# Nyström attention into a sticky top-1 MoE: the own expert of two batches chosen from the mean of C v, the first batch's steps in a new list

## The chip, the cores and the metric

The kernel runs on one core of a Trainium2 chip. The metric is the device time of one execution in microseconds; the span of the profile is the part of it in which instructions run. TensorE (PE) multiplies matrices, VectorE (DVE) does sums, transpositions and two-input arithmetic, ScalarE (ACT) exponentials and copies, GpSimd (POOL) further arithmetic, and SyncE (SP) and some of the others start DMAs.

## The reference

Eight batches with eight heads, 576 tokens and 64 columns a head. The landmarks are means of 18 tokens each, 32 a head. `sm` is a softmax over the last axis.

```python
A  = sm(q, k_lm)            # 576 x 32 a head
Bm = sm(q_lm, k_lm)         # 32 x 32
C  = sm(q_lm, k)            # 32 x 576
Z = Bm.T / (norm1(Bm) * norminf(Bm) + 1e-06)
for _ in range(6):
    Z = 2 * Z - Z @ Bm @ Z
x = A @ Z @ C @ v           # heads side by side: 512 columns a token
logits = x @ w_gate; local = sigmoid(x @ w_local)
# token by token: e = argmax(logits[s]) where s == 0 or local[s] < 0.5,
# else the expert of the token before
p = softmax(logits[s])
out[s] = p[e] * (relu(x[s] @ w1[e]) @ w2[e])   # 8 experts, 1024 inside
```

## The kernel before

Each batch has one "own" expert that is computed densely for all its 576 tokens; tokens of other experts are gathered into slots and computed at the end. In the kernel before, the own expert is the one that most tokens' gates name (`votes`: a matmul of `eq` with ones, a sum, then MAX and MAX_INDEX).

The product x·w1 is never made from x. With W = Z·(C v) of a head, the kernel forms G = W·w1 for each head (line 591, `w_w1`, from `wt`, the transposed W, and `raw`, the weights), 32 landmarks a head, and then multiplies the softmax A by it (line 634, `mm1`), in chunks f0 to f7 of 128 of the expert's 1024 columns; `mm2` (line 684, and 678 for the fifth block of 64 tokens) follows two chunks behind. A batch has two passes of eight chunks: 320 tokens (256 to 575), then 256 (0 to 255). Every number is split in a high and a low half (`gh` and `gl`, `ath` and `atl`, `wh` and `wl`), which makes three matmuls of each product. The high half is a cast by ACT, the low half a subtraction by DVE (or POOL for `wl`).

The first batch's attention runs alone (`first_attention`): its steps are written out in an order by hand, and the experts of batch 0 begin when it is over. The attention of each later batch runs beside the experts of the batch ahead, and a table (`SECOND` for batch 1, `PLANS` for 2 to 7) gives each step the chunk before which it is emitted; 16 chunks make a batch. `G_AT` gives the chunks at which the two halves of the next batch's G are emitted. All engines run their own instructions in order. A DMA is started from the queue of the engine that the code names.

Names in what follows: `sk` and `sq` are the sums that make landmarks (lines 210 and 218; the second behind a pair of POOL additions, line 214); `sa` is A with tokens on partitions, `at` its transposed form; `et` the Newton iterate, p0 to p5 its six products (line 383), each followed by a copy on ACT and an addition on DVE; `u` is C v and, in nine more columns a head group, C v times the gates' weights; `wc` is W scaled; `ad` is A in memory, from which slots are filled; `h` and `hx` are the hidden activations (`hx` of the fifth block). C's scores are line 250, A's are line 421, gates line 470. `keep_warm` multiplies zeros, to no result. PE's score banks and chain banks come from a pool named `one` in turn.

## Time and profile before

| what | us |
|---|---|
| median of 3 runs | 495.1 (494.94 to 495.57) |
| the profiled execution | 495.34 |
| its span | 493.4 |
| PE busy in the span | 469.5 (95%) |
| first matmul of an expert | at 38.09 |
| first matmul of batch 0's second pass | at 75.40 |
| first matmul of batch 1's first pass | at 104.70 |
| POOL, DVE, ACT busy | 229.0, 269.8, 215.2 |

Times in rows count from the start of the span. A row of a timeline gives the start, the time in which the group was busy, engine, line, operation, and tiles out<-in; what stands in brackets is the idle time of the engine ahead of it and what ended it.

### The profile page before, as it was taken

How to read it: one execution, taken by the hardware profiler on the slowest of the kernel's cores; microseconds unless marked ns; L12 is line 12 of the kernel's file. 1: busy time of each engine (PE TensorE's matmuls, PEld its weight loads, DVE VectorE, ACT ScalarE, POOL GpSimd, SP SyncE). 2: the span in 40 equal slices, each digit the busy share in tenths (PEclk: the TensorE clock that was granted, in tenths of full speed). 3: DMA queues.
4: the chain of work that ended last, by engine and by line, in shares of the span. 5: the costliest groups of instructions: out<-in, count | busy, mean ns of one | idle time of the engine just before them, and what ended most of it. 6: DMA issues, size and time to landing. Idle time of an engine off the chain costs nothing.

```text
span 493.4 us, 12117 instructions
## 1 busy us (share of the span) xinstructions
PE 469.5 (95%) x4699; PEld 341.6 (69%) x4701; DVE 269.8 (55%) x823; ACT 215.2 (44%) x562; POOL 229.0 (46%) x332
## 2 busy tenths in 40 slices
PE   7759999999999999899999999999999999999994
PEld 2425667677785677667776777677786787788773
DVE  6777785675467436845465445446553466363220
ACT  3417536373163713554253723465343613532451
POOL 6267682385067604762256703353242714352661
PEclk9958999999999999999999999999999999999999
DMA  8967542954079605961197306341721361191230
GB/s 297 389 240 246 193 145 63 389 192 145 1 257 336 195 0 193 324 229 44 37 400 243 109 11 230 131 163 62 266 104 44 101 252 37 60 316 42 62 130 19
DMA packets 38620, 82.57 MB, mean 167 GB/s; under 512 B 3180, under 2 KB 4460, under 8 KB 37793
## 3 DMA queue, kind: packets, MB, share of 16 engines
q1 hardware_dynamic: 30672, 66.22, 38.6%
q10 hardware_dynamic: 6400, 10.49, 5.9%
q0 software_dynamic: 1488, 5.07, 2.8%
q8 instruction: 38, 0.62, 0.5%
q14 instruction: 22, 0.17, 0.1%
HBM read 66.34 MB, written 15.47 MB: 166 GB/s over the span
## 4 chain that ended last, share of the span: by engine, by line
PE 80%; DVE 5%; DMA 4%; issue 4%; POOL 3%; ACT 2%; POOLq 0%; SPq 0%; ACTq 0%; DVEq 0%
PE py L684 33%; PE ph L634 20%; PE pg L678 6%; PE ph L591 3%; PE one L250 3%; DMA raw<-w 3%; PE one L421 3%; PE one L383 3%; PE one L289 2%; PE one L275 2%; POOL t L214 1%; PE one L470 1%; DMA k_t<-kT 1%; PE pg L591 1%; POOL wl L622 1%
## 5 line engine op out<-in xcount | busy, mean ns | idle before, releaser
L684 PE MATMUL py<-wh,h 128*128 128x512 f32 x528 | 170.2, 403 | 0.9 <-DVE h L646 0.6
L622 POOL TENSOR_TENSOR wl<-raw,wh 128x512 fp32r<-128x512 f32 x72 | 92.3, 1306 | 69.3 <-ACT wh L617 53.1
L684 PEld LDWEIGHTS py<-wh,h 128*128 128x128 f32 x528 | 94.7, 188 | 30.3 <-issue 9.8
L643 ACT ACTIVATE h<-ph 128x256 fp32r<-128x256 f32 (+2 forms) x136 | 54.0, 400 | 129.4 <-PE ph L634 117.7
L646 DVE SCALAR_TENSOR_TENSOR h<-ph,h 128x256 fp32r<-128x256 f32 (+1 forms) x136 | 55.9, 412 | 83.1 <-ACT h L643 82.3
L684 PE MATMUL py<-wl,h 128*128 128x512 f32 x264 | 88.8, 394 | 0.0
L634 PE MATMUL ph<-ath,gh 128*128 128x320 f32 (+1 forms) x256 | 80.4, 314 | 1.2 <-DVE h L646 1.1
L634 PE MATMUL ph<-atl,gh 128*128 128x320 f32 (+1 forms) x256 | 76.0, 297 | 0.0
L634 PE MATMUL ph<-ath,gl 128*128 128x320 f32 (+1 forms) x256 | 75.9, 296 | 0.0
L634 PEld LDWEIGHTS ph<-ath,gh 128*128 128x128 f32 x256 | 48.3, 189 | 18.5 <-issue 6.3
L684 PEld LDWEIGHTS py<-wl,h 128*128 128x128 f32 x264 | 49.5, 188 | 10.7 <-issue 0.3
L634 PEld LDWEIGHTS ph<-atl,gh 128*128 128x128 f32 x256 | 48.4, 189 | 3.9 <-issue 0.3
L634 PEld LDWEIGHTS ph<-ath,gl 128*128 128x128 f32 x256 | 48.4, 189 | 0.6 <-issue 0.5
L617 ACT CAST wh<-raw 128x512 fp32r<-128x512 f32 x72 | 42.6, 626 | 4.4 <-DMA raw<-w 3.9
L699 ACT ACTIVATE ys<-py,pall 128x512 f32<-128x512 f32 x32 | 21.0, 683 | 12.4 <-DMA out<-ys 6.9
L214 POOL TENSOR_TENSOR t<-q_t 128x288 f32<-128x288 f32 x28 | 22.5, 826 | 7.8 <-DVE sk L218 3.9
L433 POOL TENSOR_TENSOR sa<-sa,mxa 128x1152 f32<-128x1152 f32 x7 | 14.9, 2133 | 18.4 <-DVE mxa L432 18.4
L605 DVE TENSOR_TENSOR gl<-ph,gh 128x512 fp32r<-128x512 f32 (+1 forms) x19 | 12.5, 662 | 19.9 <-ACT gh L604 19.8
L708 POOL TENSOR_TENSOR ys<-ys,yl 64x512 f32<-64x512 f32 x8 | 10.2, 1281 | 28.0 <-ACT yl L706 28.0
L678 PE MATMUL pg<-wh,h 128*128 128x512 f32 x56 | 22.6, 403 | 0.0
L591 PE MATMUL ph<-raw,wt 64*32 64x512 f32 (+1 forms) x136 | 20.4, 604 | 2.1 <-DMA raw<-w 2.1
L678 PE MATMUL pg<-wl,h 128*128 128x512 f32 x56 | 22.1, 395 | 0.0
(300 smaller groups left out, 733.3 us busy)
## 6 DMA issues: line engine op xcount, KB each, us to landing
raw<-w SPq DMA_DIRECT2D x72, 256.0 KB, 5.6
raw<-w SPq DMA_DIRECT2D x17, 1024.0 KB, 7.1
v_t<-v SPq DMA_DIRECT2D x8, 1024.0 KB, 7.3
out<-ys ACTq DMA_DIRECT2D x32, 256.0 KB, 2.3
q_t<-qT SPq DMA_DIRECT2D x6, 1152.0 KB, 6.2
k_t<-kT SPq DMA_DIRECT2D x6, 1152.0 KB, 9.3
ad<-sa POOLq DMA_DIRECT2D x8, 576.0 KB, 5.3
q_t<-qT SPq DMA_DIRECT2D x4, 576.0 KB, 8.9
```

Source lines behind the costliest of these rows:

```text
L214: add = nc.gpsimd.tensor_add(t9[:, i], src[:, a + i, :, 0:9], src[:, a + i, :, 9:18])
L250: mms.append(nc.tensor.matmul(pc[hf][32 * c:32 * c + 32, 0:n], st["ql"][r, h // 2, :], st["k"][r, h // 2, 288 * hf:288 * hf + n], start=Tr ...
L433: nc.gpsimd.tensor_tensor(out=sa, in0=sa, in1=mx.unsqueeze(2).broadcast_to([P, 2 * NJ, M]), op=ALU.subtract)
L591: mm = nc.tensor.matmul(ps[g][32 * c:32 * c + 32, 0:n * P], st["wt"][r, g, 32 * c:32 * c + 32], w1[r, n * i:n * i + n, a * P:a * P + P], s ...
L617: cut = nc.scalar.copy(out=wh, in_=raw)
L622: nc.gpsimd.tensor_tensor(out=wl, in0=raw, in1=wh.bitcast(F32), op=ALU.subtract)
L634: mm = nc.tensor.matmul(hp, w[:, g, c], x[:, g, s0:s0 + n], start=(i == 0), stop=(i == 5))
L643: nc.scalar.activation(out=h[:, 0:e], in_=hp[:, 0:e], func=AF.Relu)
L646: nc.vector.scalar_tensor_tensor(out=h[:, 384:384 + m], in0=hp[:, 0:m], scalar=0.0, in1=h[:, 0:m].bitcast(F32), op0=ALU.max, op1=ALU.subtract)
L678: nc.tensor.matmul(yps[4], hs[ff][1], w, start=(ff == 0 and w is w2[ff][0]), stop=(ff == NC2 - 1 and w is w2[ff][1]))
L684: nc.tensor.matmul(yps[k], h[:, part + i * P:part + i * P + P], w, start=(f == 0 and part == 0 and w is wh), stop=(f == NC2 - 1 and part = ...
L699: nc.scalar.mul(out=ys, in_=yp, mul=st["pw"][:, k:k + 1])
```

## The change

- The own expert of batches 0 and 1 (`PICK = 2`) is no longer voted. The column mean of C v·w_gate over all landmarks and heads (a matmul with 32-bit ones, 16 columns) goes through a sum, MAX and MAX_INDEX. Gates, `mxl` and `eq` remain, since the slots and the weights p need them.
- `first_attention` is now a list of named steps, `FIRST`. The A of tokens 256 to 575, which the first pass needs, is made there (`as_1` to `sl1`, 10 blocks of 32 tokens, both head groups at once). The A of tokens 0 to 255 (`as_0` to `ad0`), the gates, the votes' rest and what follows on them are placed beside the experts of batch 0 by the chunks in `BESIDE`. The write of A to memory is in two parts.
- 36 single matmuls on zeros, z0 to z35, stand between the steps of `FIRST`; before, there were groups of 8 and 6.
- C v is emitted between the second and third Newton product, and W is scaled before the gates' columns are. PE's banks are named for each step by hand.
- `et` has another layout. The write of `wt` to memory for batch 0 is started on SP's queue in place of ACT's. One POOL addition no longer waits for the own expert of batch 0.
- `SECOND`, `PLANS` of all six batches, `G_AT`, `LATER` and `IN_ROW` have other numbers. The weights of the next own expert (`w1`) are asked for at the same entry as before for batches 1 and 3 (9.1 and 7.1), and 0.5 to 2.0 chunks later for the others.

Functions `scores_c8` and `gate_weights` are added but no batch uses them. In the new listing lines move: C's scores are line 252, A's 472 and 1072 (batch 0), G 667, `mm1` 710, `mm2` 760 and 754, gates 525, `wc` 450, landmark sums 215 and 220.

The core of the difference; of the tables, G_AT and IN_ROW stand for the rest:

```diff
+PICK = 2
...
-                add = nc.gpsimd.tensor_add(t9[:, i], src[:, a + i, :, 0:9], src[:, a + i, :, 9:18])
-                if b == 1 and a == i == 0:
-                    tc.add_manual_dep(add.ins, marks["expert of batch 0"], mybir.DependencyInfo(
-                        mybir.DependencyClass.Sync, mybir.DependencyReason.DATA), reason="not beside the first choice")
+                nc.gpsimd.tensor_add(t9[:, i], src[:, a + i, :, 0:9], src[:, a + i, :, 9:18])
...
+        (nc.scalar if b else nc.sync).dma_start(out=wtd[b], in_=st["wt"].rearrange("p g x -> p (g x)"))
...
+    def best(b, n):
+
+
+        top = sm.tile([P, E], F32, name="top")
+        nc.vector.max(out=top, in_=n)
+        marks[f"expert of batch {b}"] = nc.vector.max_index(out=regs[:, b, :], in_max=top, in_values=n).ins.name
...
+        largest(st)
+        if b < PICK:
+            return
...
+    def pick(b, st):
+
+
+
+        pt = one.tile([P, 2, E])
+        nc.tensor.matmul(pt, ones32, st["u"][:, :, D:D + E], start=True, stop=True)
+        tot = sm.tile([P, E], F32, name="tot")
+        nc.vector.reduce_sum(out=tot, in_=pt.rearrange("p g e -> p e g"), axis=AX.X)
+        best(b, tot)
 
...
+    FIRST = ("z18 q0 z4 z27 z5 c0 k0 q2 cm00 z3 b0 z15 z34 be0 k2 z29 warm z7 cm01 b1 z17 c1 z21 z8 ce0 z6 "
+             "be1 no0 z10 cm10 z1 z12 z24 nf0 z31 no1 cm11 z32 ce1 as_1 nf1 p0 e0 t0 d0 t2 t4 p1 z13 e1 v0 "
+             "cs at11 z23 d1 v1 z14 p2 e2 at01 z28 z33 ut z11 z26 d2 p3 am1 uwg e3 d3 pk w1 p4 z2 e4 d4 p5 "
+             "z22 z19 z20 ae1 z30 e5 an1 d5 nw ab1 sc1 z16 nwc nwg z25 nwt hq z9 z0 hk mq sl1 z35 mk G")
+    BESIDE = dict(as_0=0.1, at0=1.1, ad1=1.6, am0=1.6, ae0=2.6, an0=2.6, ab0=3.6, sc0=5.1, sl0=5.1, ad0=6.6,
+                  gates=3.6, votes=4.6, fresh=4.6, sticky=6.1, chosen=6.6, own=7.1)
+    G_AT = {0: (12, 14), 1: (14, 15), 2: (14, 15), 3: (14, 15)}
+    END = 4
+    LATER = (1.1, 2.0, 6.0, 8.0), (1.1, 2.6, 4.5, 6.5)
+    IN_ROW = 6
...
+        def a_scores(hf):
+            for g in range(2):
+                if hf:
+                    bank("ag"[g])
+                pa[g, hf] = one.tile([P, 512])[:, 0:32 * nh[hf]]
+            mms = []
+            for c in range(4):
+                for g in range(2):
                     r, a = rows(g, c)
-                    nc.tensor.matmul(pa[g, hf][32 * c:32 * c + 32, :], st["k"][r, a, S:S + M],
-                                     st["q"][r, a, 288 * hf:288 * hf + 288], start=True, stop=True)
+                    mms.append(nc.tensor.matmul(pa[g, hf][32 * c:32 * c + 32, :], st["k"][r, a, S:S + M],
+                                                st["q"][r, a, 256 * hf:256 * hf + 32 * nh[hf]], start=True, stop=True))
+            in_row(mms)
...
+        for k in range(36):
+            steps[f"z{k}"] = with_bank("h", lambda: keep_warm(1))
...
+        steps["w1"] = fetch
+        steps["G"] = lambda: w_w1(st, 0, 2)
...
-    G_AT = {0: (12, 15), 1: (14, 15), 2: (12, 14), 3: (11, 14)}
-    END = 4
-    LATER = (0.1, 2.5, 5.5, 6.5), (1.6, 2.1, 4.0, 5.5)
-    IN_ROW = 9
```

On DVE, just ahead of the first G: before, the sum of the votes, MAX, MAX_INDEX, then the scaling of W, `atl` for all tokens, landmark sums of batch 1, and the low half of G.

```order
L488 TENSOR_REDUCE tot<-one 128x8
L490 MAX top<-tot 128x8
L491 MAX_INDEX regs<-top,tot 128x8
L399 TENSOR_TENSOR wc<-ph,rc 128x256
L459 TENSOR_TENSOR atl<-at,ath 128x1152
L218 TENSOR_REDUCE sq<-t_559 128x64
L210 TENSOR_REDUCE sk<-k_t 128x64
L473 MEMSET lg 64x32
L605 TENSOR_TENSOR gl<-ph,gh 128x256 x2
L605 TENSOR_TENSOR gl<-py,gh 128x256 x2
```

Now, from the transposition of the first pass's A on:

```order
L1097 STREAM_TRANSPOSE at<-sa 128x640
L450 TENSOR_TENSOR wc<-ph,rc 128x256
L435 TENSOR_TENSOR wgc<-ph,rc 128x2x9
L220 TENSOR_REDUCE sq<-t_578 128x64
L215 TENSOR_REDUCE sk<-k_t 128x64
L1112 TENSOR_TENSOR atl<-at,ath 128x320 x2
L681 TENSOR_TENSOR gl<-ph,gh 128x256 x2
L681 TENSOR_TENSOR gl<-py,gh 128x256 x2
L220 TENSOR_REDUCE sq<-t_692 128x64
L215 TENSOR_REDUCE sk<-k_t 128x64
L1077 STREAM_TRANSPOSE sa<-one 128x256 x2
L722 SCALAR_TENSOR_TENSOR h<-ph,h 128x256
```

Votes and MAX_INDEX have left the place between W and G, `atl` is two pieces of 320 columns behind the landmark sums, and the transpositions of the early A scores stand behind a second pair of landmark sums and ahead of the first `h`.

On PE, from the end of the first chunk of expert matmuls on, before:

```order
L634 MATMUL ph<-ath,gl 128x320
L634 MATMUL ph<-ath,gh 128x320
L634 MATMUL ph<-atl,gh 128x320
L634 MATMUL ph<-ath,gl 128x320
L250 MATMUL one<-k_t,ql 32x288 x4
L250 MATMUL one<-k_t,ql 32x320 x4
L634 MATMUL ph<-ath,gh 128x320
L634 MATMUL ph<-atl,gh 128x320
```

And now:

```order
L710 MATMUL ph<-ath,gh 128x320
L710 MATMUL ph<-atl,gh 128x320
L710 MATMUL ph<-ath,gl 128x320
L1072 MATMUL one<-q_t,k_t 32x256 x8
L252 MATMUL one<-k_t,ql 32x288 x4
L252 MATMUL one<-k_t,ql 32x320 x4
L710 MATMUL ph<-ath,gh 128x320
L710 MATMUL ph<-atl,gh 128x320
L710 MATMUL ph<-ath,gl 128x320
```

Eight matmuls of A's scores for tokens 0 to 255 have come between chunk f0 and the scores of C for batch 1.

On PE, at the first half of G for batch 3, beside the experts of batch 2, before:

```order
L383 MATMUL one<-et 32x64 x8
L684 MATMUL py<-wh,h 128x512 x2
L684 MATMUL py<-wl,h 128x512
L591 MATMUL ph<-raw_2861,wt 32x512
L591 MATMUL pg<-raw_2861,wt 32x512
L591 MATMUL ph<-raw_2861,wt 32x512
L591 MATMUL pg<-raw_2861,wt 32x512
L591 MATMUL ph<-raw_2861,wt 32x512
L591 MATMUL pg<-raw_2861,wt 32x512
L591 MATMUL ph<-raw_2861,wt 32x512
L591 MATMUL pg<-raw_2861,wt 32x512
L634 MATMUL ph<-ath,gh 128x256
```

And now:

```order
L417 MATMUL one<-et 32x2x32 x8
L323 MATMUL one<-v_t,ect 32x64 x40
L417 MATMUL one<-et 32x2x32 x8
L667 MATMUL ph<-raw_2944,wt 32x512
L667 MATMUL pg<-raw_2944,wt 32x512
L667 MATMUL ph<-raw_2944,wt 32x512
L667 MATMUL pg<-raw_2944,wt 32x512
L667 MATMUL ph<-raw_2944,wt 32x512
L667 MATMUL pg<-raw_2944,wt 32x512
L667 MATMUL ph<-raw_2944,wt 32x512
L667 MATMUL pg<-raw_2944,wt 32x512
L710 MATMUL ph<-ath,gh 128x256
```

The G of batch 3 stands between the same kinds of expert work, but two chunks later (14 in place of 12, `G_AT`).

## Rows read from the trace of the kernel before

**Rows 1.** Busy time of each engine, from the page: us, share of the span, instructions.

```profile
PE 469.5 (95%) x4699; PEld 341.6 (69%) x4701; DVE 269.8 (55%) x823; ACT 215.2 (44%) x562; POOL 229.0 (46%) x332
```

**Rows 2.** Busy time by stretch of the span, PEclk the granted clock.

```profile
24.00:38.00 14.00, 8.43 (x104) 3.24 (x105) 9.36 (x25) 2.52 (x6) 8.38 (x14) 0.50 0.71 256
38.00:75.40 37.40, 36.02 (x443) 23.53 (x435) 29.24 (x86) 21.21 (x74) 28.45 (x34) 0.97 0.52 182
75.40:470.00 394.60, 391.23 (x3772) 293.27 (x3766) 209.91 (x654) 173.48 (x434) 173.66 (x234) 1.00 0.46 158
```

**Rows 3.** Timeline of PE from C v to the first scores beside experts.

```profile
17.57 0.90 PE L289 MATMUL py<-v_t,ect 128*32 128x64 f32 x40
...
20.60 0.57 PE L289 MATMUL py<-v_t,ect 128*32 128x64 f32 x17 [1.28 <-issue]
...
26.43 0.71 PE L392 MATMUL ph<-u,et 32*32 32x73 f32 x16 [0.81 <-DVE et L388]
...
31.59 0.66 PE L406 MATMUL ph<-ident,wc 128*128 128x128 f32 x2 [1.18 <-DVE wc L399]
...
35.76 1.11 PE L591 MATMUL ph<-raw,wt 64*32 64x256 f32 x16 [0.94 <-DMA raw<-w]
...
38.09 0.63 PE L634 MATMUL ph<-ath,gh 128*128 128x320 f32 x1
...
39.99 1.44 PE L250 MATMUL one<-k_t,ql 64*32 64x288 f32 x16
```

**Rows 4.** Timeline of ACT, the copy of wt.

```profile
32.29 0.37 ACT L408 COPY wt<-ph 128x256 f32<-128x256 f32 x1 [2.69 <-PE ph L406]
```

**Rows 5.** Timeline of DVE before the first expert matmul.

```profile
25.04 0.74 DVE L958 TENSOR_REDUCE rsa<-sa 128x18 f32<-128x576 f32 x1
...
30.96 0.16 DVE L491 FIND_INDEX8 regs<-top,tot 128x8 uint32<-128x8 f32 x1
31.04 0.41 DVE L399 TENSOR_TENSOR wc<-ph,rc 128x256 f32<-128x256 f32 x1
31.36 1.81 DVE L459 TENSOR_TENSOR atl<-at,ath 128x1152 fp32r<-128x1152 f32 x1
33.79 0.75 DVE L218 TENSOR_REDUCE sq<-t 128x64 f32<-128x576 f32 x1 [0.62 <-POOL t L214]
34.46 1.34 DVE L210 TENSOR_REDUCE sk<-k_t 128x64 f32<-128x1152 f32 x1
```

**Rows 6.** Timeline of POOL in the same stretch.

```profile
26.44 1.16 POOL L961 TENSOR_TENSOR sa<-sa,rsa 128x576 f32<-128x576 f32 x1 [1.38 <-DVE et L388]
...
31.21 2.54 POOL L214 TENSOR_TENSOR t<-q_t 128x288 f32<-128x288 f32 x2 [2.51 <-DVE regs L491]
...
35.00 1.43 POOL L214 TENSOR_TENSOR t<-q_t 128x288 f32<-128x288 f32 x2
```

**Rows 7.** Timeline of PE beside the first experts.

```profile
43.95 0.42 PE L634 MATMUL ph<-ath,gh 128*128 128x320 f32 x1
...
44.95 0.64 PE L684 MATMUL py<-wh,h 128*128 128x512 f32 x2
...
52.36 0.47 PE L678 MATMUL pg<-wh,hx 128*128 128x512 f32 x1 [0.40 <-DVE hx L649]
...
56.94 0.71 PE L684 MATMUL py<-wh,h 128*128 128x512 f32 x2
...
79.10 0.74 PE L470 MATMUL one<-at,wgc 128*32 128x160 f32 x16
```

**Rows 8.** PE's waits by line and releaser, 38 to 480 us.

```profile
PE one L383 <- DVE et L388: 0.6, 1, 0.6
```

**Rows 9.** Timeline of PE at the first G for batch 3.

```profile
203.28 0.61 PE L591 MATMUL ph<-raw,wt 64*32 64x512 f32 x1 [1.16 <-DMA raw<-w]
```

**Rows 10.** DMA issues from the page.

```profile
ad<-sa POOLq DMA_DIRECT2D x8, 576.0 KB, 5.3
```

More of the change, by code (lines that the diff above doesn't have):

```diff
@@ L881, in nystrom_attn_then_sticky_moe @@
     xs = {}
+    second = {}
     def done(steps):
@@ new lines, in first_attention @@
+        for g in range(2):
+            for hf in range(2):
+                steps[f"cm{g}{hf}"] = lambda g=g, hf=hf: c_max(g, hf)
+            steps[f"at{g}1"] = lambda g=g: a_turn(g, 1)
+        parts = dict(as_=a_scores, am=a_max0, ae=a_exp0, an=a_norm0, ab=a_back0, sc=cut, sl=rest)
+        for name, fn in parts.items():
+            steps[f"{name}1"] = lambda fn=fn: fn(1)
+        second.update({f"{name}0": lambda fn=fn: fn(0) for name, fn in parts.items()},
+                      at0=lambda: (a_turn(0, 0), a_turn(1, 0)), ad0=lambda: a_out(0), ad1=lambda: a_out(1))
@@ L967, in first_attention @@
+        for k in range(36):
+            steps[f"z{k}"] = with_bank("h", lambda: keep_warm(1))
+        for k in range(6):
+            gen = newton_step(0, st, k)
+            steps[f"p{k}"] = lambda gen=gen: next(gen)
+            steps[f"e{k}"] = lambda gen=gen: next(gen)
+            steps[f"d{k}"] = lambda gen=gen: done(gen)
         load(0, st)
```

323 lines of the change are left out of this document (178 added, 145 removed), and 36 rows, old and new, of the table PLANS.

## The prediction, made before the changed kernel was run

> **What bounds the kernel now.** I read the page's top first, then the busy time by stretch, then the timeline of each engine up to 60 us, then the list of TensorE's waits. TensorE (PE) is busy for 469.5 us, 95% of the span [rows 1]. By stretch it is busy in 391.2 of 394.6 us from 75.4 to 470, in 36.0 of 37.4 from 38 to 75.4, but in 8.4 of 14.0 from 24 to 38, where its granted clock is 0.50, the lower of its two levels, 1.2 GHz [rows 2]. So from the first expert matmul on, only PE work and PE stops count; before it, a chain of small steps does. The timeline of PE names that chain's end: W leaves the Newton matmuls at 26.43, the transposition for wt stands at 31.59, G starts at 35.76 with 0.94 us of waiting for the own expert's weights, the first expert matmul at 38.09 [rows 3]. VectorE (DVE) shows why: MAX_INDEX, which picks that expert from the votes, runs at 30.96 and only then the scaling of W at 31.04 [rows 5]. Both the weights and W wait behind gates and votes.
>
> The profiled execution took 495.34 us, 1.94 outside its span; the median of the runs is 0.24 below it. My sum is made against 495.34 and then shifted by that. No change means within 0.2%, 1.0 us, about what measurement can tell here.
>
> **The first choice.** The matmul with ones, the sum and MAX_INDEX now need only the columns that C v and wg give. I place MAX_INDEX behind the fifth Newton product: p4 is at 26.0 in my walk below, MAX_INDEX at 26.4. From MAX_INDEX to the first G took 35.76 − 30.96 = 4.8 us [rows 3, 5], so the weights allow G at 31.2. They no longer end last.
>
> **W instead ends last.** C v now stands behind the second Newton product (19.5 us in place of 17.57), and I let it keep the stop of 1.3 us inside it that ended at 20.60 with no releaser but "issue" [rows 3]. 20.60 − 17.57 = 3.03, so it resumes at 22.5. The third product follows at 22.9, then 24.3, 26.0 and 26.6 by the old steps. On DVE the row sums of A now stand ahead of the last Newton addition, 25.04 to 26.2 in the old rows for 18 columns [rows 5], so W is multiplied at 28.6 (26.43 before). POOL's product of A took 1.16 us for 18 columns [rows 6], 1.28 by size for 20; it ends at 29.8, its transposition at 30.7, and W's scaling, behind it on DVE, takes 0.41 [rows 5]: 31.1. Transposition at 31.6, wt's copy, 0.37 long and starting 0.70 behind the transposition as before [rows 3, 4], is done about 32.0; G 32.3. That is 3.4 earlier.
>
> The Trainium skill (page "Runtime: NRT & Kernel Launch", section "Instruction fetch mechanics") says that engines fetch blocks of instructions by themselves and that crossing a block's boundary is mostly hidden. The trace disagrees in this place if the stop is such a fetch, with 1.28 us in the open; no row says what it is. By the page's rule the stop would go and the time be 1.3 less, 492.4; by the row it stays, 493.7.
>
> **From G to the first expert matmul.** DVE has between wgc and the split of G: two sums of batch 1's landmarks, 0.75 and 1.34 [rows 5] with 0.67 between their starts, then the low half of A for 640 columns, two pieces at 320/1152 of 1.81, together 1.0 [rows 5]. The first of them waits for POOL's pair of additions: 1.43 when alone, 2.54 beside DVE's subtraction of two inputs [rows 6]. I take 1.43, since DVE does a transposition and W's scaling in that time: 29.8 + 1.4 = 31.2, sums from 31.4 to 33.4, low halves to 34.4, the low half of G 0.7 more: 35.05 against 38.09, **−3.0**. With 2.54 it is −1.9.
>
> **Clock.** The first chunk of expert matmuls took 39.99 − 38.09 = 1.90 us at the lower clock [rows 3]; the same six took 44.95 − 43.95 = 1.00 later [rows 7]. The 36 single matmuls on zeros fill PE's pauses. If the clock stays at its upper level, 0.9 goes, and by an estimate from the mean of 0.97 from 38 us on [rows 2] 0.2 of C's scores behind it: **−1.1**. If it falls as before, the pauses A and B below shrink by as much, since DVE and ACT set their ends; so it hardly touches the sum.
>
> **Work moved behind the first matmul.** The scores of A for tokens 0 to 255 (8 matmuls of 256 columns; C's 8 of 288 and 320 took 1.44 [rows 3], so 1.2 by columns, 1.0 without the lower clock's 0.2) and the gates (0.7, as those of batch 1 at 79.10 [rows 7]) stood ahead of the first expert matmul, where PE waited anyway, and now stand on its path: **+1.7**.
>
> **New pauses.** A: the second bank of C's first scores is free when DVE has transposed the early A scores; these stand behind 0.75 and 1.34 us of landmark sums: 38.5 in the walk, 0.95 idle. B: C's next scores need a bank that ACT's exponentials free at about 42.05: 1.35 idle. D: the A scores of batch 1 need the transposition of the early ones out of a buffer that is written to memory first; POOL's write is issued at about 48.3 in the walk; its landing lies between 2.4 us, by size for 256 of the 576 KB, and the group's median of 5.3 [rows 10]. I take 3.6, a third of the way up, nearer to the size than to the median, since the size is what is known: 51.9, 0.55 idle. E: the matmuls of block 4 wait for DVE's hx, 0.55. Together 3.4. The old stretch has 0.4 and 0.6 [rows 7, 8] and, by PE's idle 37.40 − 36.02 [rows 2], 1.4 in all, 0.1 of it not waits: about 1.25. **+2.15**. By the walk the third chunk's second product so starts at 56.2 in place of 56.94 [rows 7], and the gates are still to come.
>
> **Later batches.** G of batch 3 waited 1.16 us for its weights [rows 9], all alone in the stretch. It moves two chunks back. Eight chunks with 320 tokens took 37.4 us [rows 2], so two are over 7 us at 256, and its load is planned for the same time: **−1.16**. The other tables exchange attention steps within stretches where PE is busy 99% [rows 2]: 0, between −2.2 (394.60 − 391.23, all that PE idled there, less the 1.16) and +2, since an attention step placed too early waits as in [rows 8], and three such waits make 2.
>
> **Sum.** −3.0 − 1.1 + 1.7 + 2.15 − 1.16 = −1.4: 495.34 − 1.4 − 0.24 = **493.7 us**. Its own range is 492.4 (where rival 1 begins) to 494.1.
>
> **Rivals.**
> 1. Better (490.1 to 492.4). The stop in C v doesn't come back, so W is ready 1.3 us sooner (492.4); or A and B, which rest on my walk of DVE and ACT, do not fall on PE: 2.3 less (491.4); both give 490.1. For: the stop has no releaser in the trace, so nothing ties it to C v. Against: POOL's A product then ends last and takes back part.
> 2. No change (494.1 to 496.1). POOL's pair takes 2.54 as when it ran beside DVE (+1.1, 494.8), or one pause is an us longer. For: DVE has two-input subtractions for A close by.
> 3. Slower, from one mechanism: the write of batch 0's A holds the next A. POOL's write queues behind landmark additions; at 2.54 a pair in place of 1.43 for two pairs it is issued 2.2 later [rows 6], and a landing of 5.3 us [rows 10] in place of 3.6 adds 1.7. DVE's transpositions of batch 1's A wait for it, and so do all h behind them on DVE, so PE stops: +3.9, 497.6. From a landing 1.5 us later than walked there is no gain, from 2.5 it is slower. For: on the same queue a median of 5.3. Against: this write is less than half as large.
> 4. The mean picks another expert than the votes: then more tokens go to slots at the end. On the inputs given, the mean of C v and the votes name the same expert in both batches, so I give it 0.01, in the slower case.
>
> **How the numbers follow.** Forecast 0.36 (faster), better 0.24 (0.12 of it the stop alone), no change 0.22, slower 0.18. Faster 0.60, same 0.22, slower 0.18. The range is 489.8 to 496.8: 0.3 below the lower end of rival 1, since the later tables may give up to 2.2 more, and above up to where half of rival 3 is left out; about 0.15 lies outside.
>
> **What would show it.** In the changed profile: MAX_INDEX near 26.4 us; G near 32.3 with no wait for weights; first expert matmul near 35; granted clock of 24 to 38 us near 1.0; waits of C's scores for DVE and ACT between 37 and 42; one wait for the transposition of A near 52; no wait of G for weights in batch 2. Wrong if W is late (pauses between Newton steps), if DVE holds h back after 45 us, or if the gain at the first matmul is spent by 75 us.

## The result, and the profile after

The changed kernel takes 499.58 us (median of 7 runs, 497.65 to 499.92), the kernel before 495.1 beside it; the ratio is 1.0074, interval 1.0054 to 1.0093. It is slower, and the prediction was wrong in sign and range. The profiled execution took 499.80 us with a span of 497.8, 4.4 more than before.

To see where these 4.4 us lie, cut the span at the first expert matmul and at the first matmul of the slot pass (line 634 or 710 on `xah`). Busy time in the first two of the three stretches, before (the third is 19.52 long before and 19.42 after):

```profile
0.00:38.09 38.09, 25.74 (x390) 11.59 (x393) 26.67 (x73) 11.93 (x35) 18.22 (x57) 0.81 0.86 311
38.09:473.88 435.79, 431.04 (x4240) 319.30 (x4232) 240.34 (x742) 197.19 (x512) 202.89 (x269) 1.00 0.46 159
```

and after (columns as in [rows 2]; the last two rows are cut at the times of [rows 2]; the view counts a DMA packet where it starts, so a short stretch can show a DMA share above 1):

```profile
0.00:34.13 34.13, 27.42 (x387) 12.23 (x388) 21.68 (x62) 11.77 (x40) 14.55 (x52) 1.00 0.77 264
34.13:478.38 444.25, 432.03 (x4280) 321.66 (x4281) 250.82 (x756) 198.82 (x511) 206.32 (x276) 0.99 0.47 163
...
24.00:38.00 14.00, 9.61 (x164) 4.54 (x152) 10.98 (x28) 5.94 (x18) 10.17 (x13) 1.00 0.92 318
38.00:75.40 37.40, 31.26 (x370) 22.42 (x367) 29.52 (x76) 16.30 (x57) 26.51 (x33) 0.95 0.49 185
```

The start is 4.0 us shorter and no longer runs at the lower clock (1.00 where it was 0.50 from 24 to 38 us). The middle is 8.46 us longer, of which TensorE (PE) works 1.0 and idles 7.5 more. I call this middle "the stretch" below. Most of the added idle time falls from 38 to 75 us, where PE idles 6.1 us against 1.4 [rows 2]. The timeline of PE shows its pauses; each answers to a place in [rows 3, 7]:

```profile
21.11 0.66 PE L323 MATMUL py<-v_t,ect 128*32 128x64 f32 x18 [0.26 <-issue]
...
31.80 0.79 PE L667 MATMUL ph<-raw,wt 64*32 64x256 f32 x16
...
34.13 0.42 PE L710 MATMUL ph<-ath,gh 128*128 128x320 f32 x1 [1.11 <-DVE gl L681]
...
37.40 0.74 PE L252 MATMUL one<-k_t,ql 64*32 64x320 f32 x8 [1.05 <-DVE sa L1077]
...
41.64 0.47 PE L252 MATMUL one<-k_t,ql 64*32 64x320 f32 x4 [1.80 <-ACT ec L265]
...
44.89 0.55 PE L309 MATMUL one<-ident,ec 128*128 128x128 f32 x3 [0.46 <-ACT ec L265]
45.20 0.71 PE L760 MATMUL py<-wh,h 128*128 128x512 f32 x2
...
55.97 1.16 PE L472 MATMUL one<-q_t,k_t 64*32 64x288 f32 x14 [3.87 <-DVE sa L477]
57.07 1.28 PE L525 MATMUL one<-at,wgc 128*32 128x64 f32 x32
```

G starts 4.0 us sooner, but the first matmul of line 760 (684 before) at 45.20 stands no sooner than at 44.95 [rows 7]: the whole gain is spent in eleven microseconds, by 1.05, 1.80 and 0.46 of pauses and by work that stood elsewhere. Then comes a pause of 3.87. Cut at the first and third chunk's second product (44.95 and 56.94 in [rows 7]), before:

```profile
38.09:44.95 6.86, 6.86 (x66) 4.25 (x59) 6.03 (x19) 5.57 (x20) 5.34 (x7) 0.83 0.88 303
44.95:56.94 11.99, 11.26 (x98) 6.82 (x96) 9.13 (x30) 7.15 (x27) 9.38 (x11) 1.00 0.31 98
```

and after, with a cut more at the end of the long pause:

```profile
34.13:45.20 11.07, 7.75 (x87) 4.41 (x87) 8.56 (x24) 6.80 (x24) 8.31 (x8) 1.00 1.04 405
45.20:55.97 10.77, 6.90 (x45) 4.40 (x42) 10.70 (x23) 5.23 (x18) 8.68 (x10) 1.00 0.25 88
55.97:60.81 4.84, 4.84 (x72) 3.23 (x73) 4.78 (x12) 0.96 (x4) 2.58 (x3) 0.65 0.50 173
```

26.68 us in place of 18.85: 7.8 of the 8.46 arise here, PE idle for 7.2 where it was for 0.7, and behind the long pause the mean granted clock is 0.65: the lower level, 0.50, from 56.1 to 59.5 us. ACT shows the cause of the second pause:

```profile
39.68 0.62 ACT L693 CAST wh<-raw 128x512 fp32r<-128x512 f32 x1 [3.50 <-DMA raw<-w]
...
41.46 0.51 ACT L265 ACTIVATE ec<-one,nm 128x288 f32<-128x288 f32 x1
```

The exponentials that free PE's bank stand on ACT behind a cast of `w2`, and that waits for a piece of `w2` that SP asks for behind the second half of the own expert's `w1`. That order on SP is the same before. SP asks for the piece at 29.98, 5.4 sooner than before (35.40), but it takes 9.7 us to land in place of 7.9; and before, ACT comes to its cast only at 43.33, behind the exponentials `bm`, when the piece is there. The DMA share of 24 to 38 us is 0.92, against 0.71 [rows 2], and 1.04 from 34.13 to 45.20. For the pause of 3.87, DVE and POOL side by side:

```profile
48.41 0.70 POOL L1100 DMA_DIRECT2D ad<-sa  x1
49.07 1.37 POOL L698 TENSOR_TENSOR wl<-raw,wh 128x512 fp32r<-128x512 f32 x1
50.32 1.52 POOL L219 TENSOR_TENSOR t<-q_t 128x288 f32<-128x288 f32 x2
51.73 2.54 POOL L698 TENSOR_TENSOR wl<-raw,wh 128x512 fp32r<-128x512 f32 x2
57.52 0.74 POOL L219 TENSOR_TENSOR t<-k_t 128x288 f32<-128x288 f32 x1 [3.25 <-DVE sq L220]
```

```profile
49.41 5.49 DVE L1112 TENSOR_TENSOR atl<-at,ath 128x256 fp32r<-128x256 f32 x2
55.44 0.85 DVE L477 STREAM_TRANSPOSE sa<-one 128x288 f32<-128x288 f32 x2
```

Two subtractions of 256 columns stand at 5.49 us; the group of this line has 413 ns for the shorter and 5154 for the longer. The long one began at 49.4, behind POOL's write, and ended at 54.5, when POOL's unbroken run ended (51.73 + 2.54 = 54.27). Everything on DVE behind it came late, the transposition at 55.44 among it, and for that PE waited.

### The profile page after: what moved, and what is told of

Read it like the earlier page. It is cut to its first block, busy times and chain, and to the rows that moved or that the text cites. A ratio compares the mean times of both kernels' runs of the same rounds, so it can differ in the third digit from the quotient of the medians.

```text
span 497.8 us, 12220 instructions
## 1 busy us (share of the span) xinstructions
PE 472.1 (95%) x4745; PEld 344.6 (69%) x4745; DVE 275.3 (55%) x826; ACT 216.8 (44%) x565; POOL 228.7 (46%) x334
## 4 chain that ended last, share of the span: by engine, by line
PE 75%; DMA 8%; DVE 8%; POOL 4%; issue 3%; ACT 1%; SPq 0%; POOLq 0%; ACTq 0%
PE py L760 31%; PE ph L710 19%; DMA raw<-w 6%; PE pg L754 5%; PE one L472 3%; PE one L252 3%; PE ph L667 2%; PE one L417 2%; PE one L323 2%; PE one L309 2%; DVE atl L1112 1%; DMA q_t<-qT 1%; PE ph L161 1%; PE one L525 1%; POOL wl L698 1%
## 5 line engine op out<-in xcount | busy, mean ns | idle before, releaser
L760 PE MATMUL py<-wl,h 128*128 128x512 f32 x264 | 89.8, 395 | 0.0
L219 POOL TENSOR_TENSOR t<-k_t 128x288 f32<-128x288 f32 x24 | 17.4, 746 | 10.1 <-DVE sq L220 7.3
L252 PE MATMUL one<-k_t,ql 64*32 64x320 f32 (+1 forms) x224 | 18.8, 425 | 3.1 <-ACT ec L265 1.8
```

The lines of the kernel that those rows point to most:

```text
L219: nc.gpsimd.tensor_add(t9[:, i], src[:, a + i, :, 0:9], src[:, a + i, :, 9:18])
L252: mms.append(nc.tensor.matmul(pc[hf][32 * c:32 * c + 32, 0:n], st["ql"][r, h // 2, :], st["k"][r, h // 2, 288 * hf:288 * hf + n], start=Tr ...
L760: nc.tensor.matmul(yps[k], h[:, part + i * P:part + i * P + P], w, start=(f == 0 and part == 0 and w is wh), stop=(f == NC2 - 1 and part = ...
```

## The experiments

Theory: DVE's subtraction of two SBUF inputs is held by POOL (3.9 us, and 3.4 us at the lower clock behind it), and the front's gain is lost to ACT's wait for `w2`. Rivals: the tables (`PLANS`, `G_AT`) cost the later batches the time; the zeros on PE change more than the clock; the write of A lands late, as in the prediction's rival 3. "First" below is the start of the first expert matmul in the profile, 38.09 before and 34.13 after, and the stretch is 435.79 and 444.25.

**The subtraction on POOL instead of DVE**

```diff
-                nc.vector.tensor_tensor(out=al, in0=fulls[hf][:, g], in1=ah.bitcast(F32), op=ALU.subtract)
+                (nc.vector if hf else nc.gpsimd).tensor_tensor(out=al, in0=fulls[hf][:, g], in1=ah.bitcast(F32), op=ALU.subtract)
```

> The changed kernel with one edit: the low half of the early tokens' A (L1112, tokens 0 to 255) is subtracted on POOL in place of DVE. Theory 1 (DVE's subtraction with two inputs in SBUF stood 5.2 us beside POOL's back-to-back subtractions): PE's wait for the transposition of A falls from 3.9 to under 0.8 us, the clock does not fall behind it (another 0.6), the time is 495 to 496.2, ratio 0.999 to 1.002. Theory 2 (the transposition waits for the write of batch 0's A to land): the wait stays at 3 us or more, with that write as its releaser, ratio 1.006 to 1.009. Theory 3 (POOL is the engine that is short): the wait moves to wl, mm2 then waits 2 us or more, ratio above 1.004.

498.64 us, ratio 1.0045 [1.0013, 1.0076]. The wait did not go (4.39): the next operation of two SBUF inputs on DVE took the subtraction's place.

```profile
51.81 5.79 DVE L385 TENSOR_TENSOR nrc<-s 128x2 f32<-128x2 f32 x1
```

A product of two columns takes 5.79 us. POOL's run here went on from its write at 50.37 to 57.57, and the product ended at 57.60. So the length of the hold isn't set by the size of the work held.

**The same with the transposition of early A a chunk earlier**

```diff
-    BESIDE = dict(as_0=0.1, at0=1.1, ad1=1.6, am0=1.6, ae0=2.6, an0=2.6, ab0=3.6, sc0=5.1, sl0=5.1, ad0=6.6,
+    BESIDE = dict(as_0=0.1, at0=0.1, ad1=1.6, am0=1.6, ae0=2.6, an0=2.6, ab0=3.6, sc0=5.1, sl0=5.1, ad0=6.6,
```

> As e1, and the transpositions of the early A scores (at0) are emitted ahead of batch 1's landmark sums (at0 0.1 in place of 1.1). Theory 1 (pauses A and B, 1.05 and 1.80 us, come from those sums ahead on DVE): both together fall to under 1.2, the time is 1.5 to 2.5 below e1. Rival: the landmarks of batch 1 come late by as much and PE waits for C's scores of batch 1 instead: within 0.7 of e1.

498.49 us, 1.0061 [1.0035, 1.0087]; wait 4.26. The scheduler left DVE's order there as it was, so this says nothing on pause A; it repeats the first run within the intervals.

**The old tables in the changed kernel**

```diff
-    G_AT = {0: (12, 14), 1: (14, 15), 2: (14, 15), 3: (14, 15)}
+    G_AT = {0: (12, 15), 1: (14, 15), 2: (12, 14), 3: (11, 14)}
...
```

(and PLANS of before.)

> The changed kernel with the tables PLANS and G_AT of before; SECOND, LATER, IN_ROW and the first batch as changed. Theory 1 (the new tables cost: pauses of 0.9 and 1.1 us at 163 to 165 us where before had 0.6, against 1.2 gained at batch 3's G): 0 to 1.5 us below the changed kernel, 498.1 to 499.6. Rival (the tables gain the 1.2 as forecast and the pauses at 163 us come from batch 1, whose table stays): 0.5 to 1.5 above it.

500.86 us, 1.011 [1.0073, 1.0147]. The wait of batch 3's G is back with 1.54 and the 3.85 stays. The new tables are not what costs time.

**The early choice alone, in the kernel before**

```diff
+        if b == 0:
+            return
...
+    def pick(b, st):
+        pt = one.tile([P, 2, E])
+        nc.tensor.matmul(pt, ones32, st["u"][:, :, D:D + E], start=True, stop=True)
...
+        pick(0, st)
```

> The kernel before with the early choice alone for batch 0: MAX_INDEX from the mean of C v behind the fifth Newton product, no votes matmul for batch 0; all else as before. Theory 1 (W ends last, then DVE's low halves): G near 33, first expert matmul 2.3 to 3.2 us earlier than 38.09, the time 492 to 493, ratio 0.994 to 0.996. Rival (only the 0.94 us of waiting for the weights can go): ratio 0.998 to 0.999.

495.6 us, 0.999 [0.9972, 1.0009]. First came at 36.72, 1.4 sooner, C v without a stop, and it was all given back at the scores of C, where the same cast on ACT waits for `w2`:

```profile
42.37 0.69 PE L252 MATMUL one<-k_t,ql 64*32 64x288 f32 x8 [2.10 <-ACT ql L225]
...
41.03 0.62 ACT L630 CAST wh<-raw 128x512 fp32r<-128x512 f32 x1 [1.69 <-DMA raw<-w]
```

So the early choice alone is enough to lose the front's gain; none of the change's other parts is needed for it.

**The product of two columns by a column as a scalar**, on top of the first run

```diff
-        nc.vector.tensor_mul(nrc, s4[:, 0:2], s4[:, 2:4])
+        for g in range(2):
+            nc.vector.tensor_scalar(out=nrc[:, g:g + 1], in0=s4[:, g:g + 1], scalar1=s4[:, 2 + g:3 + g], scalar2=None, op0=ALU.mult)
```

> As e1 (low half of the early A on POOL), and the product of the two norms (L385, 2 columns, two tensors in SBUF), which stood 5.8 us on DVE there, is made with one tensor and a scalar a partition, so DVE has no instruction with two tensors in SBUF beside POOL's unbroken run of 51.0 to 57.6 us. Theory 1 (such an instruction waits until POOL pauses): PE's wait of 4.3 us for the transposition of A falls under 0.8; from the first expert matmul to the slot pass 436.5 to 438 us in place of 441.4 (e1, e2); ratio 0.995 to 1.000. Theory 2 (the write of A to memory must land): the wait stays at 2.5 us or more, behind the transposition itself; 440 us or more.

498.26 us, 1.0058 [1.003, 1.0086]. The two operations on one column pass; the next, one SBUF input of two columns and two constants, is held:

```profile
52.34 0.34 DVE L386 TENSOR_SCALAR nrc<-s 128x1 f32<-128x1 f32 x2
52.71 5.44 DVE L387 TENSOR_SCALAR nrc<-nrc 128x2 f32<-128x2 f32 x1
```

**The same with casts of `w2` two chunks later**

```diff
-        if i < 5:
+        if b == 0 and 2 <= i < 7:
+            cut_w2(b, i + 1)
+        if b and i < 5:
...
-        if b == 0 and i < 4:
-            cut_w2(b, NC2 - 4 + i)
```

> As e5, and the cast of the fourth piece of w2 (and those behind it) on ACT is emitted two chunks later. Theory (at the start the loads are the bound: ACT's queue stood 3.5 us for that piece, which landed at 39.7, and the landmarks of batch 1, h and C's exponentials stood behind it): the pauses of PE for C's exponentials of batch 1 (1.1 to 1.8 and 0.5 to 1.0 us) fall to 0.6 in all, first mm2 2 to 3 us after where e5 has 11 to 12 behind the first expert matmul less 1 to 2; 1 to 2 us below e5 from first expert matmul to slot pass. Rival (DVE's own queue, sums of landmarks ahead of the transpositions, sets these pauses): within 0.6 of e5.

500.1 us, 1.0087 [1.0058, 1.0117]; ACT's wait is replaced by PE's for `gl` (1.9) and `hx` (2.5), and line 387 was held again, for 3.88. The scheduler changed the order of much else, so the price of ACT's wait can't be read from it.

**Without the zeros** (z0 to z35 out of FIRST)

```diff
-    FIRST = ("z18 q0 z4 z27 z5 c0 k0 q2 cm00 z3 b0 z15 z34 be0 k2 z29 warm z7 cm01 b1 z17 c1 z21 z8 ce0 z6 "
+    FIRST = ("q0 c0 k0 q2 cm00 b0 be0 k2 warm cm01 b1 c1 ce0 "
...
```

> The changed kernel without the 36 single matmuls on zeros. Theory (PE's clock falls without them, but DVE and ACT end the pauses behind): granted clock near 0.5 before the first expert matmul, first chunk 1.9 in place of 1.1 us, first mm2 within 0.5 us of 45.2 all the same, time within 0.5 of the changed kernel. Rival (the clock is on the path): first mm2 and time 0.9 to 1.5 later. A third way: PE steps that no longer queue behind zeros come earlier, first expert matmul 0.3 to 1 us earlier.

500.9 us, 1.0121 [1.01, 1.0141]. First stood at 34.12 as with them, but the scheduler ordered DVE otherwise (a pause of 4.72 for `sa` of line 1077 in place of 1.05). The first chunk took 1.64 us in place of 1.08. POOL's write stood at 49.64 here, with one instruction behind it that ended at 51.12, and the subtraction's first piece took 1.05 us and ended 0.29 behind that. What the zeros give the whole through the clock stays open.

**No operation of that kind behind the write**, on top of the first run

```diff
-        nc.vector.reduce_max(out=s4, in_=stt, axis=AX.X)
+        nc.vector.reduce_max(out=s4[:, 0:2], in_=stt[:, 0:2], axis=AX.X, negate=True)
+        nc.vector.reduce_max(out=s4[:, 2:4], in_=stt[:, 2:4], axis=AX.X)
...
-        nc.vector.tensor_mul(nrc, s4[:, 0:2], s4[:, 2:4])
-        nc.vector.tensor_scalar(out=nrc, in0=nrc, scalar1=-1.0, scalar2=-1e-6, op0=ALU.mult, op1=ALU.add)
+        for g in range(2):
+            nc.vector.tensor_scalar(out=nrc[:, g:g + 1], in0=s4[:, g:g + 1], scalar1=s4[:, 2 + g:3 + g], scalar2=-1e-6,
+                                    op0=ALU.mult, op1=ALU.add)
```

> As e1 (low half of the early A on POOL), and in the norms neither an instruction with two tensors in SBUF nor one on a tensor with two constants: the first maxima are negated, and the product and the addition are one instruction with a scalar a partition, 1 column each, of the kind that took 0.17 us in e5 beside POOL's run. Theory 1 (a DVE instruction that needs what POOL's tensor instructions hold waits until POOL pauses): no DVE instruction over 1.4 us between 45 and 60 us, PE's wait of 3.3 to 4.4 us for the transposition of A falls under 0.8; from the first expert matmul to the slot pass 436.5 to 438.5 us in place of 441.4 (e1, e2). Theory 2 (any DVE instruction stands in that place): again 4 us or more, now in the maximum, the product or the reciprocal.

493.76 us, 0.9962 [0.9937, 0.9987]: faster than before. No operation of DVE is held for over 0.4 us from 45 to 57 us; the next one is `eq` of 128x40 at 58.18, which takes 2.06 us (0.19 alone), to the end of POOL's run behind the write (60.17). DVE's next wait in this place is the one predicted, for the write of A on its way to DRAM, and it costs PE nothing:

```profile
50.94 0.85 DVE L479 STREAM_TRANSPOSE sa<-one 128x288 f32<-128x288 f32 x2 [0.62 <-DMA ad<-sa]
```

**That, and the fourth piece of `w2` ahead of the second half of `w1`**

```diff
-            st["w1", 1] = load_w1(st["e"], 1)
             get_w2(0, 3)
+            st["w1", 1] = load_w1(st["e"], 1)
```

> As e8, and the fourth piece of w2 (256 KB) is asked for ahead of the second half of w1 (1 MB) on SP's queue. Theory (ACT's queue stood 3.5 us for that piece and the landmarks, h and exponentials behind it): ACT's wait for weights between 35 and 40 us falls under 1 us, the pauses of PE for C's exponentials of batch 1 fall from 1.1 to 3.3 in all to under 1; first mm2 1 to 2 us sooner behind the first expert matmul (11.1 in the changed kernel). Rival: the second half of w1 then lands late and the second G (41.8 in the changed kernel) waits 1 us or more, no gain.

493.38 us, 0.9951 [0.9934, 0.9967]. ACT's wait of 3.5 is gone and PE's pause 0.72 in place of 1.80, but the 0.46 behind it has become 1.52, since ACT now waits 1.92 for the fifth piece. From the first expert matmul to the first second product:

```profile
33.31:44.35 11.04, 7.75 (x86) 4.40 (x87) 8.46 (x24) 6.97 (x24) 8.28 (x8) 1.00 1.04 406
```

11.04 against 11.07, at the same DMA share: the exchange moved the wait from one piece to the next and gained nothing here. The 0.08% over the run before are within the intervals.

**The same exchange in the kernel before with the early choice**

```diff
-    sts[0]["w1", 1] = load_w1(sts[0]["e"], 1)
     get_w2(0, 3)
+    sts[0]["w1", 1] = load_w1(sts[0]["e"], 1)
```

> As e4 (the kernel before with the early choice alone), with the same exchange of loads. Theory: PE's pause of 2.1 us for the landmarks of batch 1, behind ACT's wait of 1.7 for that piece, falls under 0.6; first mm2 near 43.3 in place of 44.9, ratio 0.995 to 0.998 (e4 0.999). Rival: the second G waits for its weights instead, ratio 0.998 to 1.002.

494.6 us, 0.9976 [0.9964, 0.9988]. The pause of 2.10 is gone (0.37 in its place) and from first, 35.80 here, to the first second product it takes 6.46 us where the fourth run took 8.14. In this kernel, with its first expert matmul 2.5 us later than in the ninth run, the exchange keeps the gain up to there, 2.7 us by the two profiles; by the medians some 1.2 are left in the end. The early choice with the exchange is worth 0.24%.

**The comparison `eq` by five scalars**, on top of the ninth run

```diff
-        nc.vector.tensor_tensor(out=st["eq"], in0=lg8, in1=mx.unsqueeze(2).broadcast_to([P, NBLK, E]), op=ALU.is_equal)
+        for k in range(NBLK):
+            nc.vector.tensor_scalar(out=st["eq"][:, k], in0=lg8[:, k], scalar1=mx[:, k:k + 1], scalar2=None, op0=ALU.is_equal)
```

> As e9, and the comparison that marks the best expert (eq, 128x40, two tensors in SBUF, 2.06 and 2.26 us on DVE beside POOL in e9, 0.20 alone) is five instructions with one tensor and a scalar a partition, 8 columns each. Theory (such an instruction does not wait for POOL): eq takes under 1.2 us in all wherever it stands, PE's wait of 1.27 us at 61 us for the Newton addition behind it falls under 0.5, and that of 0.37 at 150 us goes; 1 to 1.6 us below e9, ratio 0.991 to 0.994. Rival (a scalar instruction on more than one column waits like the one in e5): eq 2 us or more, no gain.

500.39 us, 1.0093 [1.0067, 1.012]. Scalars on eight columns are held too, once for 2.20 and once for 0.81 us, so the rival was right that nothing is gained. These holds don't make up the 6 to 7 us by which the median is longer; where those come from isn't shown, since the profiled execution, 496.68, was the fastest one.

**The ninth run with the old tables** (PLANS of before too)

```diff
-    G_AT = {0: (12, 14), 1: (14, 15), 2: (14, 15), 3: (14, 15)}
+    G_AT = {0: (12, 15), 1: (14, 15), 2: (12, 14), 3: (11, 14)}
```

> As e9, with the tables PLANS and G_AT of before: the tables by themselves. Theory (they are worth the wait of batch 3's G, 1.16, as the prediction had it): that wait comes back at 1.0 to 1.6 us, from the first expert matmul to the slot pass 1 to 2 us longer than e9's 436.9. Rival (their other changes cost as much as they give): within 0.5 of e9.

498.16 us, 1.0058 [1.0032, 1.0083]; the stretch is 443.24 against 436.89. The wait of batch 3's G is back with 1.78 us, more than the 1.16 I gave the tables. The rest of the 6 us between these two profiles is not shown to be theirs: 2.2 of it arise up to the third second product, where the two programs have the same order on all four engines (the first difference stands at some 93 us). By the medians the tables are worth 4.1 to 4.8 us here, but 1.3 with the hold (run 3 against the changed kernel, intervals overlapping).

**A useless product of two columns in the kernel before, beside a long run of POOL**

```diff
+        if b == 0:
+            two = sm.tile([P, 2], F32, name="two")
+            nc.vector.tensor_tensor(out=two, in0=s[:, 0, 0:2], in1=s[:, 0, 2:4], op=ALU.mult)
```

> The kernel before with one instruction added that nothing needs: a DVE product of two tensors in SBUF, 2 columns, behind the reciprocal of batch 0's weights (at 44.2 us, beside POOL's run that lasts to 54.0). Theory 1 (it waits until POOL pauses): it stands 6 to 10 us, PE waits 4 us or more for h behind it, ratio 1.008 to 1.020. Rival (such an instruction costs 0.15 us and the 5 us of the changed kernel have a cause of its own): within 0.2%.

495.12 us, 0.9989 [0.9975, 1.0002]. Not held, though POOL ran without a pause from 39.75 to 53.9:

```profile
44.77 0.17 DVE L555 TENSOR_TENSOR two<-psum 128x2 f32<-128x2 f32 x1
```

The product began 0.15 us before one of POOL's instructions ended (44.92), so this run can't show a wait to the end of one instruction; a wait to the end of POOL's run it would have shown. With this "beside a busy POOL" alone fell as an explanation of the long holds. What all the holds of 3.9 us and more had in common, and this run lacks, is POOL's own issue of a DRAM write at the head of its run.

**The subtraction back on DVE in the ninth run's kernel, and that kernel once more**

```diff
-                (nc.vector if hf else nc.gpsimd).tensor_tensor(out=al, in0=fulls[hf][:, g], in1=ah.bitcast(F32), op=ALU.subtract)
+                nc.vector.tensor_tensor(out=al, in0=fulls[hf][:, g], in1=ah.bitcast(F32), op=ALU.subtract)
```

> As e9 and e15, but the low half of the early A is back on DVE, as the change has it; this is the one edit. Theory 1: its first piece stands 4 to 6 us beside POOL's run, PE waits 3 to 4.5 us for the transposition of A, 3 to 5 us above e15. Rival (the norms' product was the one that cost, and the subtraction only took its place): under 1.5 above e15.

> The kernel of e9 again, for e14 beside it: 436.9 us from the first expert matmul to the slot pass in e9, ratio 0.993 to 0.998; by the theory below both kernels.

497.5 us (1.0043 [1.0029, 1.0058]) and 494.02 (0.9976 [0.9954, 0.9999]): that one line costs 3.5 us; it stands at 5.50 us again and PE waits 3.84.

**The write of A from SP instead of POOL**, as the only edit to the changed kernel

```diff
-            nc.gpsimd.dma_start(out=ad[0:P * 2 * NJ].rearrange("(p g j) l -> p g j l", p=P, g=2)[:, :, 8 * hf:8 * hf + nh[hf]],
+            (nc.gpsimd if hf else nc.sync).dma_start(out=ad[0:P * 2 * NJ].rearrange("(p g j) l -> p g j l", p=P, g=2)[:, :, 8 * hf:8 * hf + nh[hf]],
```

> The changed kernel with one edit: the write of the first half of batch 0's A is issued by SP instead of POOL. POOL's other work about it stays the same unbroken run. If POOL's own issue of a write is what makes DVE's two-input subtraction wait to the end of the run, its first piece now takes at most 2.8 us (it took 5.15), the wait of the gate matmuls falls from 3.87 to under 1.5, and the time to about 497. If any unbroken run of POOL does it, the first piece takes 4.5 to 5.5 again and the time stays at 499 to 501. The order that the scheduler wrote differs from the gates on, so only the stretch up to them is compared.

493.51 us, 0.9965 [0.994, 0.9989]. First stands at 33.96, the stretch is 437.26, 7.0 less than after. POOL:

```profile
47.03 1.46 POOL L219 TENSOR_TENSOR t<-k_t 128x288 f32<-128x288 f32 x2
48.46 1.29 POOL L698 TENSOR_TENSOR wl<-raw,wh 128x512 fp32r<-128x512 f32 x1
49.71 1.83 POOL L219 TENSOR_TENSOR t<-q_t 128x288 f32<-128x288 f32 x2
51.49 2.54 POOL L698 TENSOR_TENSOR wl<-raw,wh 128x512 fp32r<-128x512 f32 x2
```

and DVE beside it:

```profile
49.44 1.49 DVE L1112 TENSOR_TENSOR atl<-at,ath 128x256 fp32r<-128x256 f32 x2
...
51.05 0.83 DVE L477 STREAM_TRANSPOSE sa<-one 128x288 f32<-128x288 f32 x2
51.81 0.99 DVE L385 TENSOR_TENSOR nrc<-s 128x2 f32<-128x2 f32 x1
```

POOL's run is the same without its first instruction, and longer (to 55.45). The two subtractions now take 0.60 and 0.97 us in place of 0.41 and 5.15, the product of two columns 0.99 and the step of two constants behind it 0.67: each ends about 0.3 us or less behind the POOL instruction that was running when it began, so DVE comes in between POOL's instructions here. From DVE's transposition on the order on DVE is another one (on PE only from 68 us on), and what this gave or took is not known from this run.

**The same edit to the ninth run's kernel**

> The best version so far (subtraction on POOL, the pair of maxima by a pointer, fourth piece of w2 ahead of the second half of w1) with the write of the first half of A issued by SP. The next wait there was 0.62 on that write's way to DRAM and back: if POOL's queue delayed it, the wait goes and the time is 492.5 to 494; if not, 493.5 to 495, and if SP's queue holds it behind loads of w2 the wait of the second batch's A grows to 1 to 3 us.

494.17 us, 0.9979 [0.9956, 1.0001]: no gain over the kernel without it, as nothing was held there.

**A's write on SP, and a write from POOL, in its old place, that nobody reads**

```diff
+    spare = dram.tile([P * 2 * NJ, M], F32, name="spare")
...
+            if hf == 0:
+                nc.gpsimd.dma_start(out=spare.rearrange("(p g j) l -> p g j l", p=P, g=2)[:, :, 0:nh[0]],
+                                    in_=sh[0].rearrange("p (g j) l -> p g j l", g=2))
```

> The kernel of the last run (A's write on SP) plus a write from POOL, at its old place, of the same half of A to DRAM that nobody reads. On DVE, PE and POOL the order of the instructions is then that of the changed kernel again, row for row. If POOL's own issue of a write is what holds DVE's subtraction, it comes back although nothing waits for this write: first piece 4.5 to 5.5 us, gates waiting 3 to 4, time 498 to 501. If it was the order of the instructions, or A's way over DRAM, that made the run with SP fast, the first piece stays under 2.8 us and the time at 493 to 496 in the second case; in the first it comes back too, and the two stay mixed.

498.15 us, 1.0064 [1.0036, 1.0092]. DVE, PE, POOL and ACT have the changed kernel's order again, and the hold is back, 5165 ns for the first piece:

```profile
48.24 0.69 POOL L1104 DMA_DIRECT2D spare<-sa  x1
48.91 1.36 POOL L699 TENSOR_TENSOR wl<-raw,wh 128x512 fp32r<-128x512 f32 x1
...
51.57 2.54 POOL L699 TENSOR_TENSOR wl<-raw,wh 128x512 fp32r<-128x512 f32 x2
```

```profile
49.23 5.50 DVE L1116 TENSOR_TENSOR atl<-at,ath 128x256 fp32r<-128x256 f32 x2
```

PE waits 3.9 for it. Both writes, A's from SP at 46.90 and the useless one, land 2.5 us after their issue, by 50.8 at the latest, and the subtraction needs neither; it ends at 54.4. So the landing (the prediction's rival 3) is excluded as the hold's cause. The order could still have had a part in run 16's speed. That the hold comes and goes with POOL's write is shown from both sides at this place. No run separates the write itself from the 0.6 to 0.7 us by which its issue moves POOL's instructions against DVE's.

Two rows keep this from being a rule. In the fourth run POOL ran without a gap behind its write of A (28.58) up to 32.7 us, and DVE's subtraction of 1152 columns beside it took its own time; there a POOL instruction of 0.25 us stood 1.42:

```profile
31.25 1.34 DVE L461 TENSOR_TENSOR atl<-at,ath 128x1152 fp32r<-128x1152 f32 x1
...
31.29 1.42 POOL L512 TENSOR_TENSOR eqd<-eq,desc 128x40 f32<-128x40 bf16 x1
```

And in the changed kernel `eq`, 0.19 us alone, is held over three POOL instructions (142.24 to 145.79) with no write at their head:

```profile
143.62 2.23 DVE L538 TENSOR_TENSOR eq<-lg,mxl 128x40 bf16<-128x40 f32 x1
...
142.24 2.12 POOL L484 TENSOR_TENSOR sa<-sa,mxa 128x1152 f32<-128x1152 f32 x1
144.33 1.46 POOL L219 TENSOR_TENSOR t<-q_t 128x288 f32<-128x288 f32 x2
```

So what decides whether DVE comes in between two POOL instructions stays open; a write at the head is neither enough nor needed.

The best versions, by their medians, are the ninth run (493.38, repeated 494.02), the one with A's write on SP (493.51) and the eighth (493.76); these do not differ by more than their intervals. The sixteenth needs one line.

## Why the prediction was wrong

**The start, −3.0: right, and too small in the profiled execution.** First came 4.0 sooner there. The choice was made at 25.74 (26.4 forecast), G at 31.80 (32.3), wt is the last to come, as said. The stop in C v, the cause that I had left open, was 0.26 in place of 1.28, and there was none in the kernel before with only the choice moved. It is at most a part of the difference, since W was only 0.35 sooner than forecast (28.25, 28.6 forecast). So the Trainium skill's rule (page "Runtime: NRT & Kernel Launch", section "Instruction fetch mechanics": mostly hidden) was nearer than the row. What the stop is, no run showed. A single profile tells the start poorly: runs 9 and 15 are one kernel and have their first expert matmul at 33.31 and 36.15, with spans of 489.6 and 492.9.

**The clock, −1.1: right.** 24 to 38 us were at 1.00, and the first chunk took 35.21 − 34.13 = 1.08 against 1.90 [rows 3]. Of the 14 later profiles with the same zeros and steps four (runs 1, 2, 15 and 17) have 0.76 there, so the clock's gain is not had in every execution.

**Moved work, +1.7: the sum right by luck.** 0.45 for the early scores by the pitch of the timeline (35.21 to 35.66) and 1.21 for the gates (57.07 to 58.28), 1.66, where the forecast had 1.0 and 0.7. The gates ran at the lower clock behind the long pause, which by the pitch of [rows 7] is some 0.5 of it; at the upper clock the two make 1.1 or so.

**The pauses, +2.15: the step that failed.** A was 1.05 (0.95 forecast) and E did not come. B was 1.80 (1.35), with 0.46 behind it; my walk of ACT let its cast of `w2` go on time. It overlooked that the piece, asked for 5.4 us sooner, takes longer to land (9.7 us, 7.9 before), and that ACT now comes to this cast at 36.2, ahead of the `h` and the exponentials that PE needs, where before it stood behind them. The fourth run shows it: the early choice alone gains 1.4 and gives all of it back. Exchanging two loads keeps the gain there up to the first second product (tenth run) but not in the changed kernel (ninth), where the experts start sooner still and the DMA share is 1.04; that the loads themselves then are the limit is argued from that share, not tried.

D is the term that failed: forecast at 0.55, it was 3.87, which is 3.3 of the 5.8 us by which the sum missed the profiled execution. In its chain I had the right waiters (DVE's transposition, then the scores of A) behind the wrong event: I priced the landing of the write between 2.4 and 5.3 us (and a third of the way up is 3.4, not 3.6, which is 0.2 of the 0.55) and took the subtraction `atl` on DVE at its size, though [rows 6] shows a POOL pair at 2.54 in place of 1.43 beside that very kind of operation. Measured, one piece of `atl` stood 5.15 us in place of 0.41, and the landing cost nothing. Rival 3 even gives nearly the measured time, 497.6, but by another mechanism, and the last run excludes that one. What counted at this place was where the write is issued: with POOL's own issue at the head of POOL's instructions DVE was held to their end, without it to the end of one. The chance of 0.18 for slower was too low for a stretch where POOL, DVE and a POOL write were moved beside each other. Two of the prediction's own signs of being wrong came: DVE holds `h` back after 45 us, and the gain at the first matmul is spent by 75 us.

**Later batches, −1.16: gained at batch 3's G; the whole is not clear.** Batch 3's G no longer waits for weights, as predicted. The list of PE's waits from 75 us on, after, shows what else is there:

```profile
PE ph L710 <- DVE h L722: 1.4, 1, 1.4
PE ph L667 <- DMA raw<-w: 1.1, 2, 0.9
PE py L760 <- ACT h L719: 1.1, 1, 1.1
PE one L913 <- DMA xa<-ad,gi: 0.8, 1, 0.8
...
PE ph L710 <- DVE gl L681: 0.2, 1, 0.2
PE py L760 <- DVE h L722: 0.2, 1, 0.2
```

With one more of 0.2 that is 5.0; the same list of before sums to 3.5, 1.2 of it batch 3's. So between these two profiles +1.5 in place of −1.16. But two of the waits, 0.93 for a load of G at 162.71 and 1.09 for ACT's h at 164.89, come and go between executions. In runs 1, 2, 14 and 18, which have the hold, neither is there (what PE waits at that place is 0.5 us at most); run 5 has the first (0.90), and run 8, which has no hold, has both (1.01 and 1.12). Run 18 has the changed kernel's order on all four engines, so neither the hold nor the order accounts for them. Without the two, the list sums to 3.0: some −0.5.

**The sum.** The start gave 4.0, the stretch took 8.46 and the end gave 0.1: +4.4. In the stretch PE idles 6.5 more up to the third second product (7.2 against 0.7) and 1.0 more later; the rest, 1.0, is PE's own work: 1.66 moved there and some 0.5 for the chunk at the lower clock behind the hold, less the 0.8 that the clock gives in the first chunk, and 0.4 less later. Taking the hold away gave 3.5 us in the pair of runs 14 and 15, 4.6 between the medians of runs 18 and 16, and 6 in run 16 against the changed kernel, where the order also changed; the last turned 1.0074 into 0.9965. So without that write on POOL's queue the change does shorten the kernel by about what I forecast (1.7 us in run 16, 1.4 forecast), with another order from the transposition on and a start that was more than forecast.

## What to carry to other kernels

When a plan puts work on DVE beside a busy POOL, don't take it at its size: look at the traces for operations of its kind there, and look what heads POOL's unbroken run. At one place here, behind POOL's own DMA write, a two-column product cost as much as the rest of that run. Try such writes from a queue whose engine does not compute, or keep two-input and multi-column scalar operations of DVE out of the run behind them. When a choice is made earlier, list the loads that it starts earlier, and what on each engine then waits for them in front of other work. And profile one kernel twice before reading a stretch of a single profile: runs 9 and 15 differ by 2.8 us at the first expert matmul and by 3.3 in the span, though their medians differ by 0.6.
